# Attention block beside an MLP on one core: which engine empties the second fill bank and which copies the attention output

## The chip, the cores and the metric

The kernel runs on one core of a Trainium2 chip. The core has a matrix engine (TensorE, PE in the profile; its weight loads are shown apart as PEld), a vector engine (VectorE, DVE), an activation engine (ScalarE, ACT), a general engine (GpSimd, POOL) and a queue engine that issues transfers (SyncE, SP). Each engine works through its own list of instructions in order and waits at the head of that list when something it needs is not ready. The metric is the time of one execution on the device in microseconds (us), as the median of several runs.

## What is computed

The input x has 2048 tokens of 512 values. It is layer-normalised; one branch is sliding-window attention with 32 heads of 16 values, the other a normalised MLP with a gate; the result is x plus their product.

```python
xn = layernorm(x)
q, k, v = split(xn @ wqkv)                       # 32 heads, head size 16
scores = q @ k.T * 16 ** -0.5                    # only 0 <= i - j < 256
s = softmax(scores) @ v                          # then (...) @ wo
h = gelu(layernorm(xn) @ w1 + b1)                # 512 -> 1792
g = silu(h @ w2 + b2)                            # 1792 -> 512
out = x + (s @ wo) * g
```

Products are made as three passes over a high and a low part of each operand (`PASSES`, L67), so that the result keeps more bits than one pass gives.

## The kernel before, in words

**Slots.** The attention part is written as one loop over 128 slots, `for t in range(-16, end + 1)` (L816). The heads are handled in 8 groups of 4 (n), and the tokens in 16 blocks of 128 (qb or kb), so slot t stands for group t // 16 and block t % 16. Within a group of four heads the heads go in two pairs, p = 1 and p = 0. Every engine's instructions stay in the order in which the program issues them (L32 to L46), so the order inside a slot is the order on each engine:

1. `prob_block(t, p = 1)` (L548): TensorE makes the scores of one key block against three query blocks into the tile `stb` (two banks of PSUM, the memory that TensorE writes); ScalarE takes their exponentials into a tile `pt`; GpSimd zeroes what lies outside the window (the selects). The scores are 384 columns wide, in the last two blocks of a group 256 and 128.
2. `max_block` (L496) for the slot 12 ahead (`LEAD`, L27): TensorE makes scores into `xy`, VectorE writes the far block from `zo` into it (`copy_predicated`) and takes the row maxima (`tensor_reduce`).
3. `fill_in(t, 0)` (L809): fill matmuls, see below. Then what is planned for the slot by number (`at`).
4. `prob_block(t, p = 0)`: the same as 1, into the same `stb`. So TensorE can only write it when ScalarE has done the exponentials of p = 1.
5. `fill_in(t, 1)`, then `first_scores` (L487) into `zo` for the next slot's maxima.
6. `pv_step` (L570) for the slot before: 24 small matmuls gather probabilities times values into `otb`, a 128-column part of `zo` (L195). A copy moves `otb` to the tile `oraw` (L581), of which every fourth is sent to memory.
7. What is put behind the slot (`behind`), transfers above all.

Line 581 also carries an order for the buffers of `pt` (8 of them, so four slots deep, L64): this copy is made to wait for the exponentials and selects of the slot three back (L582 to L585), so that ScalarE's next exponential, behind it, may write in their place.

**Fill pairs.** TensorE's spare time in the slots is filled with the projections of later groups (`pair_qk`, L363), the values of the second half of the heads (`pair_v`, L413) and the first MLP products (`pair_h`, L425). `tandem` (L440) runs two such jobs at once, in two PSUM banks fb0 and fb1, one job on the upper and one on the lower 64 rows of the array, over slots t0 to t1. The next pair normally starts in slot t1 + 1 with both banks, so both have to be emptied by then. That is done in slot t1, in `fill_in(t1, 0)`: ScalarE copies fb0, VectorE copies fb1 (L470, L471). VectorE's copy stands behind its maxima of slot t1. There are 22 pairs. 20 of them end below slot 116 (the last with 12 slots to go), at t1 = 8, 14, 19, 24, 30, 35, 41, 47, 53, 58, 63, 68, 74, 79, 84, 90, 98, 104, 110 and 115 (L736 to L744). Slots 14, 30 and 110 have scores of 256 columns, 47, 63 and 79 of 128; the other fourteen have 384.

For `pair_qk` the copy goes into a buffer `pjr` of a pool of five (L58), is rounded to a high part `sh` by ScalarE in a later slot, and the rest is subtracted by GpSimd; both are sent by transfers into the rows of the tile `qk` from which scores are made. For `pair_h` the copy `hr` goes to memory. For `pair_v` it goes straight into `vt`.

After slot 128 come the rest of the MLP, the output projection and the gate, which the change does not touch.

Of the kernel before, what the change touches and what calls it, by code (L numbers as in the profile page):

```python
# [18 lines left out]
P = 128  # L19
# [4 lines left out]
NQ = H // 4  # L24
EPS = 1e-5
NEG = -3.0e38
LEAD = 12  # L27
EARLY = 10
ORDER = mybir.DependencyInfo(mybir.DependencyClass.Sync, mybir.DependencyReason.DATA)
# [21 lines left out]
def mixer_kernel(ctx, tc, x, wqk, wv, wo, w1, b1, w2, b2, out):  # L51


    nc = SimpleNamespace(**{name: Ordered(tc, name) for name in ("tensor", "vector", "scalar", "gpsimd", "sync")})
# [140 lines left out]
    otb = zo[:, 1, 256:384]  # L195
    psf = attn.enter_context(tc.tile_pool(name="psf", bufs=1, space=PSUM))
    fb = [psf.tile([P, 512], F32, name=f"fb{i}") for i in range(2)]
# [92 lines left out]
    fills = {}  # L290
# [116 lines left out]
        taken.add(t)  # L407
        return t

    taken = set()  # L410
    among = {}

    def pair_v(i):  # L413
# [26 lines left out]
    def tandem(t0, t1, one, two, mid=None, back=None):  # L440

        n = one[0]
        lo, hi = slice(0, 64), slice(64, P)
        mid = mid or max(1, (t0 + t1 + 1) // 2)
        most = n // 4

        def places(slots, last):

            last = min(most, n // (len(slots) + 1)) if last else 0
            cuts = [(n - last) * k // len(slots) for k in range(len(slots) + 1)]
            out = []
            for t, a, b in zip(slots, cuts, cuts[1:]):
                ahead = min(b - a, 5 * n // 12) if t < 16 * NQ - LEAD else min(b - a, max(most, (b - a + 1) // 2))
                out += [(t, 0)] * ahead + [(t, 1)] * (b - a - ahead)
            return out + [(t1, 0)] * last

        first, second = places(range(t0, mid), False), places(range(back or mid, t1), True)
        for phase, where in enumerate((first, second)):  # L460
            for i in range(n):
                flags = dict(start=(phase == 0 and i == 0), stop=(phase == 1 and i == n - 1), skip_group_check=True)
                def unit(i=i, phase=phase, flags=flags):
                    made = ((two if phase == 0 else one)[1](fb[1 - phase], i, hi, **flags),
                            (one if phase == 0 else two)[1](fb[phase], i, lo, **flags))
                    if phase == 1 and i == 0 and t0 < 16 * NQ - LEAD:
                        for r in made:
                            tc.add_manual_dep(r.ins, outs["copy"].ins.name, ORDER, reason="the banks change rows")
                fills.setdefault(where[i], []).append((unit, ()))
        fills.setdefault((t1, 0), []).append((one[2], (fb[0], t1, nc.scalar.copy)))  # L470
        fills[t1, 0].append((two[2], (fb[1], t1, nc.vector.tensor_copy)))  # L471

    def spread(jobs, places):

# [93 lines left out]
    outs = {}  # L568

    def pv_step(n, qb):  # L570

        lo = max(qb - 2, 0)
        for kb in range(lo, qb + 1):
            for j in range(4):
                nc.tensor.matmul(otb[32 * j: 32 * j + DH + 1], vt[:, kb, (4 * n + j) % 16],
                                 pts[n, kb, j // 2][:, j % 2, P * (qb - kb): P * (qb - kb + 1)],
                                 start=(kb == lo), stop=(kb == qb),
                                 skip_group_check=True, tile_position=(0, 32 * j))
        if qb % 4 == 0:
            outs[0] = sgp.tile([P, 512], F32, tag="or", name=f"oraw_{n}_{qb}", bufs=2)  # L580
        outs["copy"] = nc.scalar.copy(outs[0][:, P * (qb % 4): P * (qb % 4 + 1)], otb)  # L581
        old = 16 * n + qb - 2  # L582
        if old >= 0:
            for w in writers[old // 16, old % 16, 0] + writers[old // 16, old % 16, 1]:
                tc.add_manual_dep(outs["copy"].ins, w.ins.name, ORDER, reason="the next slot writes in its place")  # L585
        if qb % 4 == 3:
            (at if n or qb > 7 else behind)(16 * n + qb + 2, nc.sync.dma_start, oT_d[n // 2, n % 2::2, :, P * (qb - 3): P * (qb + 1)], outs[0])

# [112 lines left out]
    n, raw = raws["qk"]  # L701
# [32 lines left out]
    fills[0, 1].insert(0, fills[0, 0].pop())  # L734
    soon = {}
    tandem(3, 8, pair_qk(1, 2), pair_qk(1, 3))  # L736
    for n, spans in enumerate((((9, 14), (15, 19)), ((20, 24), (25, 30)), ((31, 35), (36, 41)), ((42, 47), (48, 53, 51)),
                               ((75, 79), (80, 84)), ((85, 90), (93, 98))), 2):
        for c, span in zip((0, 2), spans):
            tandem(*span[:2], pair_qk(n, c), pair_qk(n, c + 1), *span[2:])  # L740
    for i, (t0, t1) in enumerate(((54, 58), (59, 63), (64, 68), (69, 74))):
        tandem(t0, t1, pair_v(2 * i), pair_v(2 * i + 1))
# [73 lines left out]
    for t in range(-16, end + 1):  # L816
# [25 lines left out]
        if t >= 1:  # L842
            pv_step((t - 1) // 16, (t - 1) % 16)
# [34 lines left out]
    for f in range(6, NF, 2):  # L878
        t = gp.tile([P, 2, 512], F32, tag="ohl", name=f"hr_{f}", bufs=4)
# [453 lines left out]
```

## Time and profile before

| what | value |
|---|---|
| median of 3 runs | 746.3 us (746.1 to 747.39) |
| profiled execution, its own time | 746.44 us |
| its span, first to last instruction | 744.7 us |
| VectorE busy | 516.5 us (69%) |
| ScalarE busy | 439.8 us (59%) |
| GpSimd busy | 298.6 us (40%) |
| granted TensorE clock | 0.999 |
| attention slots 0 to 127 | about 62 to 430 us |

The profile is of one execution. In lists of instructions a row gives the start and the duration in us, the engine, the operation, what is written and read, the shapes, and how many like it are merged; a bracket tells how long the engine sat idle before it and what ended that. Lists by group give the count, the busy time in us, the mean of one in ns, and the idle time before. A list of waits gives the total in us, the number of times and, where there is a third number, the longest.

### The profile page before, as it was taken

How to read it: one execution, taken by the hardware profiler on the slowest of the kernel's cores; microseconds unless marked ns; L12 is line 12 of the kernel's file. 1: busy time of each engine (PE TensorE's matmuls, PEld its weight loads, DVE VectorE, ACT ScalarE, POOL GpSimd, SP SyncE). 2: the span in 40 equal slices, each digit the busy share in tenths (PEclk: the TensorE clock that was granted, in tenths of full speed). 3: DMA queues.
4: the chain of work that ended last, by engine and by line, in shares of the span. 5: the costliest groups of instructions: out<-in, count | busy, mean ns of one | idle time of the engine just before them, and what ended most of it. 6: DMA issues, size and time to landing. Idle time of an engine off the chain costs nothing.

```text
span 744.7 us, 18740 instructions
## 1 busy us (share of the span) xinstructions
PE 728.3 (98%) x7360; PEld 587.2 (79%) x7360; DVE 516.5 (69%) x790; ACT 439.8 (59%) x744; POOL 298.6 (40%) x644
## 2 busy tenths in 40 slices
PE   8999999999999999999999999999999999999997
PEld 7886777777778888777776688788888888888886
DVE  6886777877776678887772577656658855676643
ACT  7757767867667676778877856443544734442001
POOL 7413757757666555767867600020102000001102
PEclk9999999999999999999999999999999999999999
DMA  8633356666555625656735385746453222254711
GB/s 294 188 71 78 86 136 149 188 173 190 147 133 154 152 71 152 156 135 168 199 102 159 102 285 196 196 142 194 109 109 113 98 87 74 68 182 116 218 50 57
DMA packets 84025, 105.71 MB, mean 142 GB/s; under 512 B 36640, under 2 KB 36896, under 8 KB 83936
## 3 DMA queue, kind: packets, MB, share of 16 engines
q1 hardware_dynamic: 83936, 104.50, 49.8%
q8 instruction: 58, 0.95, 0.5%
q14 instruction: 31, 0.25, 0.1%
HBM read 54.53 MB, written 32.77 MB: 117 GB/s over the span
## 4 chain that ended last, share of the span: by engine, by line
PE 87%; DMA 4%; ACT 4%; DVE 3%; issue 1%; POOL 1%; SPq 1%; DVEq 0%; ACTq 0%
PE fb L43 19%; PE acc L43 17%; PE zo L43 12%; PE p L43 9%; PE stb L43 9%; PE s L43 6%; PE h L43 6%; PE xy L43 5%; PE pv L43 3%; ACT pt L43 3%; DMA w<-rden_d 1%; POOL pt L43 1%; SPq L43 1%; DVE xy L43 1%; DMA qk<-qk 1%
## 5 line engine op out<-in xcount | busy, mean ns | idle before, releaser
L43 POOL TENSOR_SCALAR_AFFINE_SELECT pt<-pt 128x256 f32<-128x256 f32 x480 | 193.8, 428 | 131.7 <-ACT pt L43 127.5
L43 ACT ACTIVATE pt<-stb 128x768 f32<-128x768 f32 (+1 forms) x244 | 188.7, 773 | 56.0 <-PE stb L43 50.3
L43 DVE TENSOR_REDUCE mt<-xy 128x4 f32<-128x1024 f32 (+1 forms) x128 | 152.6, 1192 | 4.4
L43 DVE COPY_PREDICATED xy<-upper,zo 128x512 f32<-128x512 int32 x112 | 77.8, 695 | 69.9 <-PE xy L43 60.9
L43 POOL TENSOR_TENSOR xo<-xo,gated 128x512 f32<-128x512 f32 x15 | 20.0, 1331 | 237.3 <-DVE gated L43 195.7
L43 PE MATMUL fb<-xnT,wqb 64*128 64x512 f32 (+1 forms) x684 | 105.2, 399 | 0.4
L43 PE MATMUL zo<-pt,vt 128*17 128x128 f32 x2880 | 103.7, 275 | 0.3 <-POOL pt L43 0.3
L43 PE MATMUL stb<-qk 64*128 64x384 f32 (+1 forms) x488 | 94.6, 383 | 6.0 <-ACT pt L43 4.3
L43 PE MATMUL acc<-w,gh 128*128 128x512 f32 x320 | 98.6, 389 | 0.8 <-ACT gh L43 0.8
L43 PEld LDWEIGHTS stb<-qk 64*128 64x128 f32 x488 | 45.8, 183 | 47.6 <-ACT pt L43 41.4
L43 PEld LDWEIGHTS zo<-pt,vt 128*17 128x17 f32 x2880 | 67.5, 97 | 15.7 <-issue 5.7
L43 PEld LDWEIGHTS fb<-xnT,wqb 64*128 64x128 f32 (+1 forms) x684 | 64.6, 185 | 11.9 <-DVE pjr L43 1.6
L43 PEld LDWEIGHTS acc<-w,gh 128*128 128x128 f32 x320 | 60.0, 188 | 13.5 <-ACT gh L43 1.2
L43 PE MATMUL acc<-w,gl 128*128 128x512 f32 x160 | 62.3, 390 | 1.0 <-DVE gl L43 1.0
L43 PE MATMUL xy<-qk 64*128 64x256 f32 (+2 forms) x536 | 58.3, 291 | 0.2 <-DVE mt L43 0.2
L43 ACT COPY oraw<-zo 128x128 f32<-128x128 f32 x128 | 34.1, 267 | 35.2 <-PE zo L43 23.8
L43 PEld LDWEIGHTS xy<-qk 64*128 64x128 f32 x536 | 46.6, 185 | 6.7 <-issue 3.4
L43 PE MATMUL s<-wos,ohl 128*128 128x512 f32 (+1 forms) x204 | 44.3, 376 | 0.0
L43 ACT ACTIVATE gated<-acc 128x512 f32<-128x512 f32 x16 | 8.7, 596 | 59.3 <-DVE acc L43 59.3
L43 PEld LDWEIGHTS s<-wos,ohl 128*128 128x128 f32 x204 | 36.8, 188 | 7.1
L43 PEld LDWEIGHTS zo<-qk 64*128 64x128 f32 x448 | 37.6, 185 | 5.0 <-DVE xy L43 1.8
L43 ACT COPY p<-p 128x512 f32<-128x512 f32 x21 | 12.3, 585 | 48.6 <-PE p L43 41.3
(191 smaller groups left out, 1235.2 us busy)
## 6 DMA issues: line engine op xcount, KB each, us to landing
qk<-sh SPq DMA_DIRECT2D x128, 128.0 KB
qk<-pjr SPq DMA_DIRECT2D x64, 128.0 KB
oT_d<-oraw SPq DMA_DIRECT2D x32, 256.0 KB
w_d<-in_w_dram SPq DMA_DIRECT2D x14, 512.0 KB
x<-in_x_dram SPq DMA_DIRECT2D x16, 256.0 KB
or<-oT_d SPq DMA_DIRECT2D x16, 256.0 KB
w<-rden_d SPq DMA_DIRECT2D x16, 256.0 KB
xo<-in_x_dram SPq DMA_DIRECT2D x16, 256.0 KB
```

The source lines that it names most:

```text
L43: r = issue(*args, **kwargs)
```

## The change

In the 20 slots in which a pair ends below slot 116, two copies change engine and place. The copy of the second bank fb1 goes from VectorE, ahead of the p = 0 exponentials, to ScalarE, behind them (`fill_in(t1, 1)`). The copy of that slot's `otb` goes from ScalarE to VectorE. The order that protects the `pt` buffers moves from the `otb` copy to the new copy of fb1, since it has to stand on ScalarE. The two pairs that end at 116 or later, 121 and 127, stay as they were.

```diff
-    taken = set()
+    taken, ends_pair = set(), set()
...
         fills.setdefault((t1, 0), []).append((one[2], (fb[0], t1, nc.scalar.copy)))
-        fills[t1, 0].append((two[2], (fb[1], t1, nc.vector.tensor_copy)))
+        if t1 >= 16 * NQ - LEAD:
+            fills[t1, 0].append((two[2], (fb[1], t1, nc.vector.tensor_copy)))
+            return
+        ends_pair.add(t1)
+
+        def copy(dst, src):
+            outs["second"] = nc.scalar.copy(dst, src)
+        fills.setdefault((t1, 1), []).append((two[2], (fb[1], t1, copy)))
...
-        outs["copy"] = nc.scalar.copy(outs[0][:, P * (qb % 4): P * (qb % 4 + 1)], otb)
-        old = 16 * n + qb - 2
+        t = 16 * n + qb + 1
+        by = nc.vector.tensor_copy if t in ends_pair else nc.scalar.copy
+        outs["copy"] = by(outs[0][:, P * (qb % 4): P * (qb % 4 + 1)], otb)
+        last = outs["second" if t in ends_pair else "copy"]
+        old = t - 3
         if old >= 0:
             for w in writers[old // 16, old % 16, 0] + writers[old // 16, old % 16, 1]:
-                tc.add_manual_dep(outs["copy"].ins, w.ins.name, ORDER, reason="the next slot writes in its place")
+                tc.add_manual_dep(last.ins, w.ins.name, ORDER, reason="the next slot writes in its place")
```

On ScalarE the list of such a slot was: exponentials p = 1, copy of fb0, exponentials p = 0, copy of `otb`. It becomes: exponentials p = 1, copy of fb0, exponentials p = 0, copy of fb1. On VectorE the copy of fb1 (128 x 512) gives way to the copy of `otb` (128 x 128). In the built program the order of every other instruction on all engines is the same, apart from which buffer of the pool of five some tiles get. In slot 8 ScalarE also rounds the first bank's copy right behind the new copy.

## Prediction

> **What bounds the kernel now.** I read the page first, then the list of waits, then the places of the 20 slots in order of time. The page says that TensorE is the engine that is never free; the waits say what still holds it up.
>
> ```profile
> PE 728.3 (98%) x7360; PEld 587.2 (79%) x7360; DVE 516.5 (69%) x790; ACT 439.8 (59%) x744; POOL 298.6 (40%) x644
> ```
> ```profile
> PEld stb L43 <- ACT pt L43: 41.4, 144, 0.7
> ```
> ```profile
>   DVE pjr L43: 1.9, 9
>   DVE hr L43: 0.9, 3
>   DVE vt L43: 0.2, 1
> ```
>
> The second row is the loop of the attention: TensorE waits for ScalarE's exponentials before it can write `stb` again. The last three (waits at the fill matmuls, by the tile fb) are what this change can reach: 3.0 us in 13 cases in which a new pair stood waiting for VectorE's copy of fb1. Idle time of the weight loads is not yet lost time, so I went to the slots themselves. Slot 41, where a pair ends, and slot 42:
>
> ```profile
> 183.07 0.59 ACT L43 COPY pjr<-fb 128x512 f32<-128x512 f32 x1
> 183.17 1.23 DVE L43 TENSOR_REDUCE mt<-xy 128x4 f32<-128x1024 f32 x1
> ...
> 183.55 0.82 ACT L43 ACTIVATE pt<-stb 128x768 f32<-128x768 f32 x1
> ...
> 184.31 0.68 DVE L43 COPY pjr<-fb 128x512 f32<-128x512 f32 x1
> ...
> 184.52 0.27 ACT L43 COPY oraw<-zo 128x128 f32<-128x128 f32 x1 [0.15 <-PE zo L43]
> 184.53 0.36 PEld L43 LDWEIGHTS xy<-qk 64*128 64x128 f32 x4
> ...
> 184.90 0.81 ACT L43 ACTIVATE pt<-stb 128x768 f32<-128x768 f32 x1
> 185.04 0.76 PEld L43 LDWEIGHTS fb<-xnT,wqb 64*128 64x128 f32 x8 [0.15 <-DVE pjr L43]
> ...
> 185.19 0.70 DVE L43 COPY_PREDICATED xy<-upper,zo 128x512 f32<-128x512 int32 x1 [0.21 <-PE xy L43]
> ...
> 186.46 0.81 ACT L43 ACTIVATE pt<-stb 128x768 f32<-128x768 f32 x1 [0.74 <-PE stb L43]
> ```
>
> VectorE is in its maxima until 184.40, copies fb1 until 184.99, and the fill starts at 185.04. A slot without that wait and with the same 8 fill matmuls is slot 43:
>
> ```profile
> 187.43 0.36 PEld L43 LDWEIGHTS xy<-qk 64*128 64x128 f32 x4
> 187.72 0.78 PEld L43 LDWEIGHTS fb<-xnT,wqb 64*128 64x128 f32 x8
> ```
> ```profile
> 187.80 0.81 ACT L43 ACTIVATE pt<-stb 128x768 f32<-128x768 f32 x1
> 189.17 0.81 ACT L43 ACTIVATE pt<-stb 128x768 f32<-128x768 f32 x1 [0.56 <-PE stb L43]
> ```
>
> From the `xy` loads to the fill it takes 0.29 us there, 0.51 in slot 42; from the first to the second exponentials 1.37 there, 1.56 in slot 42. So the wait costs up to 0.19 us in that slot. Of a gap between exponentials about 1.35 is the loop's own least (183.55 to 184.90), whatever the fill does; what lies above it can be won.
>
> **ScalarE's new copy.** Let X be the start of the p = 0 exponentials in the ending slot. When can the copy start, and when is ScalarE free for the next exponentials? Rows with a copy out of PSUM right behind exponentials:
>
> ```profile
> 307.88 0.82 ACT L43 ACTIVATE pt<-stb 128x768 f32<-128x768 f32 x1
> ...
> 308.58 0.27 ACT L43 COPY oraw<-zo 128x128 f32<-128x128 f32 x1
> ```
>
> The copy starts 0.70 after the exponentials, 0.12 before they end. In slot 41 the exponentials follow the fb0 copy by 183.55 - 183.07 = 0.48. So the new copy runs from X + 0.70 to X + 1.29 (0.59 as fb0's), the fill may go at X + 1.34 (0.05 from copy to fill, as 184.99 to 185.04), and ScalarE is free at X + 1.18. The next exponentials need their scores and start at X + 1.35, so the copy is hidden in ScalarE's gap with 0.17 to spare; without that cover it would cost its whole 0.59 less the 0.27 taken away, 0.32 a pair or 6.4 us in 20. The copy has its waits met: fb1's last matmul lies before the p = 0 exponentials, the selects and exponentials of three slots back are old, and its buffer's transfers were done where VectorE came to it:
>
> ```profile
> L43 DVE COPY pjr<-fb 128x512 f32<-128x512 f32 x13 | 8.8, 680 | 0.0
> ```
>
> (idle before: 0.0.) Behind it in ScalarE's queue stand the next exponentials, and for these TensorE waits.
>
> [...]
>
> **VectorE's new copy.** No row shows a 128 x 128 copy out of PSUM on VectorE. It lies above the transpose of 32 columns (202 ns) and below the 680 ns of the wide copy; I take 0.29 us, near ScalarE's 267 ns for the same shape, the nearest row.
>
> ```profile
> L43 DVE STREAM_TRANSPOSE mT<-mh 128x32 f32<-128x32 f32 x30 | 6.1, 202 | 0.7 <-POOL mh L43 0.7
> L43 ACT COPY oraw<-zo 128x128 f32<-128x128 f32 x128 | 34.1, 267 | 35.2 <-PE zo L43 23.8 <-POOL pt L43 4.0 <-POOL mh L43 2.4
> ```
>
> It waits for the matmuls into `otb`, behind which ScalarE's copy started at 184.52; VectorE's maxima end at 184.40, so it is done near 184.8. Behind it stand a small transpose in some slots and the next `copy_predicated`, which needs `xy` and starts at 185.19; TensorE needs `otb` only a slot later. So it costs nothing at either end of its range: even at 0.68 VectorE is as busy as now. VectorE's load falls by some 20 x 0.39 = 7.8 us, ScalarE's rises by 6.4. Nothing else moves in the queues of SP and GpSimd; their transfers of these copies only become ready earlier.
>
> **The sum, by three kinds of slots.** Wide scores (384): fill from X + 1.34 in place of where it starts now. Slot 41: 183.55 + 1.34 = 184.89 against 185.04, so 0.15. The first and the last of this kind:
>
> ```profile
> 134.83 0.82 ACT L43 ACTIVATE pt<-stb 128x768 f32<-128x768 f32 x1
> ...
> 136.35 0.76 PEld L43 LDWEIGHTS fb<-xnT,wqb 64*128 64x128 f32 x8 [0.19 <-DVE pjr L43]
> ```
> ```profile
> 396.41 0.82 ACT L43 ACTIVATE pt<-stb 128x768 f32<-128x768 f32 x1
> ...
> 397.90 0.19 PEld L43 LDWEIGHTS fb<-yh,xnT 64*128 64x128 f32 x2 [0.41 <-DVE hr L43]
> ```
>
> They give 0.18 and 0.15. There are nine (24, 35, 41, 53, 58, 74, 98, 104, 115), read the same way at 0.12 to 0.18: 9 x 0.14 = 1.3 us. In the five others (8, 19, 68, 84, 90) the next fill does not wait or the next gap is already the loop's least; slot 8 has the wait, but slot 9 reads
>
> ```profile
> 89.40 0.81 ACT L43 ACTIVATE pt<-stb 128x768 f32<-128x768 f32 x1
> 90.74 0.81 ACT L43 ACTIVATE pt<-stb 128x768 f32<-128x768 f32 x1 [0.53 <-PE stb L43]
> ```
>
> 1.34: nothing to win. Narrow scores (256; slots 14, 30, 110): the exponentials are shorter, so the copy comes earlier, while VectorE's maxima are as long as ever. Slot 14 and an unhindered narrow slot:
>
> ```profile
> 104.93 0.60 ACT L43 ACTIVATE pt<-stb 128x512 f32<-128x512 f32 x1
> ...
> 105.82 0.30 PEld L43 LDWEIGHTS xy<-qk 64*128 64x128 f32 x4
> ...
> 106.42 1.00 PEld L43 LDWEIGHTS fb<-xnT,wqb 64*128 64x128 f32 x10 [0.30 <-DVE pjr L43]
> ```
> ```profile
> 245.13 0.30 PEld L43 LDWEIGHTS xy<-qk 64*128 64x128 f32 x4
> ...
> 245.36 0.79 PEld L43 LDWEIGHTS fb<-wva,xnT 64*128 64x128 f32 x12
> ```
>
> Copy from 104.93 + 0.48 (0.60 less the overlap) to 106.00, fill at 106.05; TensorE is ready 0.23 after the `xy` loads, also 106.05. Against 106.42 that is 0.37, and 3 x 0.36 = 1.1. Scores of 128 (47, 63, 79):
>
> ```profile
> 200.10 0.39 ACT L43 ACTIVATE pt<-stb 128x256 f32<-128x256 f32 x1
> ...
> 200.99 0.36 PEld L43 LDWEIGHTS xy<-qk 64*128 64x128 f32 x4
> ...
> 201.59 0.76 PEld L43 LDWEIGHTS fb<-xnT,wqb 64*128 64x128 f32 x8 [0.24 <-DVE pjr L43]
> ```
>
> The copy would be done by 201.0, so the fill goes 0.29 after `xy`, at 201.28: 0.3 each. Slot 79 has two casts on ScalarE behind it that fill the gap, so I count 47 and 63: 0.6. The sum is 1.3 + 1.1 + 0.6 = 3.0 us off the profiled execution's 746.44, which is 0.1 above the median: 743.4. What follows in the loop is timed from the slot before it, so I expect nothing to be given back; next in line is the loop of `stb` and exponentials itself.
>
> **Rivals.** *The wait only changes its name* (time 746.3). In the chain of waits slot 42 shows no gap, the fill follows the `xy` matmuls at once:
>
> ```profile
> 184.86 0.24 PE xy L43 x4
> 185.10 1.15 PE fb L43 x8
> ```
>
> If the weight loads alone waited, nothing is won. Against it: 1.56 against 1.37 for the same work. The same comes out if copy and exponentials do not overlap: with 0.05 at each handing over, the next exponentials would start at X + 0.82 + 0.05 + 0.59 + 0.05 = X + 1.51. The five slots at the loop's least lose 0.16 each (0.8), the nine lose 0.03 (fill at 1.51 against 1.48, 0.3), the narrow ones still win 3 x 0.2 + 2 x 0.3 (1.2): 746.3. [...]
>
> *The copy stands at ScalarE's head and holds up the exponentials* (749). It takes over waits that the `otb` copy had: the row above has 4.0 us of idle time put down to selects (POOL pt). It decides from the point where the copy starts later than X + 0.87, where the case without overlap comes out even; each 0.1 us beyond is 0.1 in 20 slots, 2 us. At 0.14 beyond, X + 1.01, it is 2.8 us slower. For it: ScalarE's idle gap is only 0.17 wide. Against it: those selects are three slots old, and the idle rows lie where `otb` itself ends.
>
> **Chances.** Forecast 0.62, nothing won 0.24 (0.14 for the name alone, 0.10 for no overlap), slower 0.14. About 0.2% or 1.5 us is what a measurement of this kernel can tell from no change; the forecast is beyond that. Faster 0.62, same 0.24, slower 0.14. If the whole of the delay at the fills goes (0.19 to 0.22 in the nine), the sum is 3.7, so 742.2 with a little for the run; above, the range takes in the second case and the start of the third: 742.2 to 747.2.
>
> **What would show it.** Right: the fill rows by tile fb wait for neither VectorE nor ScalarE beyond a tenth; the fb1 copies on ScalarE start 0.70 behind the exponentials; gaps from X to the next exponentials stay at 1.35; the gaps one slot on fall from 1.56 to about 1.41; in slot 15 the fill starts 0.23 behind the `xy` loads, not 0.60; VectorE's 20 narrow copies take near 0.29. Wrong: idle time at fb1 copies on ScalarE, gaps of 1.4 to 1.5 at the pair's end, or fill waits put down to ACT.

## The result and the profile after

The changed kernel takes **742.66 us** (median of 6 runs, 742.09 to 743.89) against 746.22 for the kernel before in the same session (6 runs, 744.93 to 747.53): a ratio of 0.9951, with a 95% interval of 0.9937 to 0.9965, so 3.6 us less. The profiled execution took 742.66 us, with a span of 740.9 where before it was 744.7, at a granted clock of 0.998.

The page of the changed kernel, its engines' row, and from its list of waits the loop's own wait:

```profile
PE 724.8 (98%) x7360; PEld 586.4 (79%) x7360; DVE 509.9 (69%) x790; ACT 444.0 (60%) x744; POOL 297.8 (40%) x644
```
```profile
PEld stb L43 <- ACT pt L43: 41.6, 143, 0.7
```

TensorE is busy 3.5 us less with the same 7360 matmuls (3.0 of it in slots 0 to 127), so the time that rows of matmuls cover is not work alone. The wait for the exponentials is what it was, 41.6 us against 41.4: the change did not touch the loop of scores and exponentials. In the waits at the fill matmuls (by the tile fb of the changed kernel) the three VectorE rows are gone. Two waits for a copy of fb are left, both for ScalarE:

```profile
  ACT hr L43: 0.5, 2
```

One of them, at 421.3, belongs to the pair that ends in slot 127. The other is that of slot 115, which the change does reach: its fill waits 0.27 us for ScalarE's copy, where it waited 0.41 for VectorE's (397.90 in the rows of the prediction).

```profile
394.20 0.19 PEld L43 LDWEIGHTS fb<-yh,xnT 64*128 64x128 f32 x2 [0.27 <-ACT hr L43]
```

The groups by shape of the changed kernel show the copies at their new places (count, busy us, mean ns, idle before):

```profile
L43 ACT COPY oraw<-zo 128x128 f32<-128x128 f32 x108 | 28.7, 266 | 30.9 <-PE zo L43 18.8 <-POOL pt L43 4.7 <-POOL mh L43 3.5
L43 ACT COPY pjr<-fb 128x512 f32<-128x512 f32 x28 | 16.5, 590 | 3.1 <-PE fb L43 1.8 <-DMA qk<-qk 0.4
L43 DVE COPY oraw<-zo 128x128 f32<-128x128 f32 x20 | 5.8, 290 | 2.0 <-PE zo L43 0.8
```

Slots 41 and 42 of the changed kernel, in order of time:

```profile
181.38 0.59 ACT L43 COPY pjr<-fb 128x512 f32<-128x512 f32 x1
...
181.86 0.82 ACT L43 ACTIVATE pt<-stb 128x768 f32<-128x768 f32 x1
...
182.56 0.59 ACT L43 COPY pjr<-fb 128x512 f32<-128x512 f32 x1
182.80 0.29 DVE L43 COPY oraw<-zo 128x128 f32<-128x128 f32 x1
...
183.21 0.79 PEld L43 LDWEIGHTS fb<-xnT,wqb 64*128 64x128 f32 x8
183.32 0.81 ACT L43 ACTIVATE pt<-stb 128x768 f32<-128x768 f32 x1 [0.16 <-PE stb L43]
...
184.67 0.81 ACT L43 ACTIVATE pt<-stb 128x768 f32<-128x768 f32 x1 [0.54 <-PE stb L43]
```

With X = 181.86 the second bank's copy runs from X + 0.70 to X + 1.29, and the fill starts at X + 1.35 with no wait in its row. VectorE has emptied `otb` at 183.09, 0.47 before the next `copy_predicated` (183.56). In this one slot the scores came 0.1 late (next exponentials at X + 1.46; in the other eight of its kind 1.35 to 1.38), so the gain of slot 42 (1.56 to 1.35 from one exponentials to the next) is in part taken back here. TensorE waits there for a transfer (last section). Slots 14 and 15 of the changed kernel, the narrow kind:

```profile
104.74 0.60 ACT L43 ACTIVATE pt<-stb 128x512 f32<-128x512 f32 x1
...
105.23 0.59 ACT L43 COPY pjr<-fb 128x512 f32<-128x512 f32 x1
...
105.63 0.30 PEld L43 LDWEIGHTS xy<-qk 64*128 64x128 f32 x4
...
105.87 0.99 PEld L43 LDWEIGHTS fb<-xnT,wqb 64*128 64x128 f32 x10
```

The fill stands 0.24 behind the `xy` loads; it was 0.60 (105.82 to 106.42 in the rows of before).

To put the gain in places I took the time from the first exponentials of an ending slot to those two slots later, after less before, and summed it by the prediction's kinds; "rest" is every other slot of the 128. These columns are against the first profile of before; each ratio is to runs of before of the same session, with medians from 745.56 to 746.22. The last two kernels are told of under "What lies outside the pairs".

| kernel | median us, ratio to before [95%] | nine wide | six narrow | five at the loop's least | rest |
|---|---|---|---|---|---|
| the change | 742.66, 0.9951 [0.9937, 0.9965] | -1.20 | -1.92 | +0.18 | -0.67 |
| fb1_only | 743.59, 0.9964 [0.9952, 0.9976] | -1.24 | -1.97 | +0.31 | -0.67 |
| otb_only | 746.04, 1.0004 [0.9994, 1.0014] | +0.04 | +0.20 | +0.35 | -0.86 |
| fb1_ahead | 748.81, 1.0039 [1.0024, 1.0055] | +1.98 | -0.41 | +2.12 | -0.46 |
| narrow_only | 743.6, 0.9969 [0.996, 0.9978] | -0.06 | -2.16 | -0.03 | -0.09 |
| wide_only | 744.1, 0.998 [0.9971, 0.9989] | -0.91 | -0.18 | +0.27 | -0.41 |
| fb1_twice | 753.62, 1.0106 [1.009, 1.0123] | +4.67 | +1.24 | +3.17 | -0.95 |
| best1 | 742.14, 0.9954 [0.9941, 0.9966] | -0.70 | -1.96 | +0.06 | -0.32 |
| before, second profile | one run, 746.3 | -0.04 | +0.03 | -0.03 | -0.16 |
| before_plus2 | 746.44, 1.001 [0.9999, 1.0022] | -0.02 | -0.14 | +0.06 | -0.47 |
| before_plus5 | 746.06, 1.0003 [0.9994, 1.0013] | +0.23 | +0.05 | +0.19 | -0.47 |

The pairs of the change sum to -2.93 us, where the prediction had 3.0. The rest, -0.67, it did not have.

### The profile page after: what moved, and what is told of

The parts are those of the page before. It is cut to its first block, busy times and chain, and to the rows that moved or that the text cites. A ratio compares the mean times of both kernels' runs of the same rounds, so it can differ in the third digit from the quotient of the medians.

```text
span 740.9 us, 18755 instructions
## 1 busy us (share of the span) xinstructions
PE 724.8 (98%) x7360; PEld 586.4 (79%) x7360; DVE 509.9 (69%) x790; ACT 444.0 (60%) x744; POOL 297.8 (40%) x644
## 4 chain that ended last, share of the span: by engine, by line
PE 86%; DMA 4%; ACT 4%; DVE 3%; SPq 1%; POOL 1%; issue 1%; DVEq 0%; ACTq 0%
PE fb L43 18%; PE acc L43 18%; PE zo L43 13%; PE p L43 9%; PE stb L43 9%; PE s L43 6%; PE h L43 6%; PE xy L43 5%; PE pv L43 3%; ACT pt L43 3%; DMA qk<-sh 1%; DMA w<-rden_d 1%; SPq L43 1%; POOL pt L43 1%; DMA qk<-qk 1%
## 5 line engine op out<-in xcount | busy, mean ns | idle before, releaser
L43 PEld LDWEIGHTS stb<-qk 64*128 64x128 f32 x488 | 45.9, 183 | 48.4 <-ACT pt L43 41.6
L43 ACT COPY oraw<-zo 128x128 f32<-128x128 f32 x108 | 28.7, 266 | 30.9 <-PE zo L43 18.8
L43 ACT COPY p<-p 128x512 f32<-128x512 f32 x21 | 12.3, 584 | 48.6 <-PE p L43 41.4
```

The lines of the kernel that those rows point to most:

```text
L43: r = issue(*args, **kwargs)
```

## The experiments

The theory: in the slot where a pair ends, the fill of the next pair waits for the second bank; with ScalarE's copy behind its exponentials the fill can start 0.14 to 0.36 us sooner than with VectorE's behind its maxima, and ScalarE has just room for it. The rivals: the gain is VectorE's lighter load or the move of `otb`; or it is somewhere else than in the pairs. The diffs are against the changed kernel unless said otherwise.

**Each half alone.** In fb1_only the `otb` copy stays on ScalarE, behind the new copy:

```diff
-        by = nc.vector.tensor_copy if t in ends_pair else nc.scalar.copy
+        by = nc.scalar.copy
...
-        last = outs["second" if t in ends_pair else "copy"]
+        last = outs["copy"]
```

> The fb1 copy goes to ScalarE behind the p = 0 exponentials as in the change, but the otb copy stays on ScalarE behind it. My theory (the gain is the fill's shorter wait for fb1): fills start as in the change, X + 1.35 in wide slots and X + 1.13 or 1.2 in narrow ones; ScalarE's list is 0.18 longer in the gap, so the next exponentials move from X + 1.35 to between X + 1.36 and X + 1.40 in 14 wide slots: 743 to 743.5 us, at least three quarters of the gain. Rival (the gain is otb going to VectorE, out of ScalarE's way): the gain is gone, 746. Rival (the gain is VectorE's lighter load): VectorE loses 13.6 us instead of 7.8, so as fast as the change or faster, 742 to 742.7.

In otb_only the second bank goes back to VectorE ahead of the p = 0 exponentials, and the order of the `pt` buffers to the copy of the first bank:

```diff
-        fills.setdefault((t1, 0), []).append((one[2], (fb[0], t1, nc.scalar.copy)))
+        def copy(dst, src):
+            outs["second"] = nc.scalar.copy(dst, src)
+        fills.setdefault((t1, 0), []).append((one[2], (fb[0], t1, copy)))
+        fills[t1, 0].append((two[2], (fb[1], t1, nc.vector.tensor_copy)))
         if t1 >= 16 * NQ - LEAD:
-            fills[t1, 0].append((two[2], (fb[1], t1, nc.vector.tensor_copy)))
             return
         ends_pair.add(t1)
-
-        def copy(dst, src):
-            outs["second"] = nc.scalar.copy(dst, src)
-        fills.setdefault((t1, 1), []).append((two[2], (fb[1], t1, copy)))
```

> Only the otb copy changes to VectorE in the 20 slots; the fb1 copy stays on VectorE behind its maxima. The order for the pt buffers is moved to ScalarE's fb0 copy. My theory: fills start as before (X + 1.49), nothing won; VectorE has 0.29 more in front of its next maxima, 0 to 0.1 in each of 20 slots: 746 to 747.5 us. Rival (otb out of ScalarE's way is the gain): 743 to 744.

fb1_only took 743.59 us, a ratio of 0.9964 [0.9952, 0.9976]; otb_only 746.04, 1.0004 [0.9994, 1.0014]. So the gain is that of the earlier copy of fb1, and the move of `otb` brings nothing by itself. A lighter VectorE is not the gain either: in fb1_only it copies neither in these slots, and the time is no shorter than that of the change.

otb_only is not a clean half. With the order on the copy of fb0, ScalarE's sequencer goes through two more waits ahead of that copy, and the p = 0 exponentials come up to 0.18 us later behind those of p = 1 (in slot 41 1.54, where before has 1.41). The fill of the next pair is not moved by that: in slot 41 it starts 2.90 behind the p = 1 exponentials in both kernels, so it still goes by VectorE's copy.

Slot 41 in fb1_only:

```profile
181.83 0.82 ACT L43 ACTIVATE pt<-stb 128x768 f32<-128x768 f32 x1
182.53 0.59 ACT L43 COPY pjr<-fb 128x512 f32<-128x512 f32 x1
183.00 0.30 ACT L43 COPY oraw<-zo 128x128 f32<-128x128 f32 x1
183.17 0.76 PEld L43 LDWEIGHTS fb<-xnT,wqb 64*128 64x128 f32 x8
183.18 0.83 ACT L43 ACTIVATE pt<-stb 128x768 f32<-128x768 f32 x1
```

Even both copies fit: the second starts 0.47 behind the first, at X + 1.17, and the exponentials follow at X + 1.35 as in the change. Only in slot 8, where ScalarE rounds a copy in the same gap as well, does it cost: the next exponentials come at X + 1.85, in the change at X + 1.69 (1.70 before). The move of `otb` to VectorE is cover for such a slot, and the runs show no more of it: the intervals of fb1_only and of the change overlap, and their pairs sum to -2.90 and -2.93.

**The copy ahead of the exponentials.** ScalarE copies both banks one after the other between p = 1 and p = 0:

```diff
-        fills.setdefault((t1, 1), []).append((two[2], (fb[1], t1, copy)))
+        fills[t1, 0].append((two[2], (fb[1], t1, copy)))
```

> As the change, but ScalarE copies fb1 right behind fb0, ahead of the p = 0 exponentials. VectorE's load is that of the change. My theory: the fill never waits, but the exponentials come 0.48 later in all 20 slots; nine wide slots lose 0.48 - 0.2, five lose 0.48, six narrow ones lose about 0.12: 751 to 752.5 us. Rival (VectorE's lighter load is the gain): 742 to 743.

It took 748.81 us, 1.0039 [1.0024, 1.0055]. Slot 41 of fb1_ahead, with the two copies in one row:

```profile
182.63 0.81 ACT L43 ACTIVATE pt<-stb 128x768 f32<-128x768 f32 x1
...
183.56 1.07 ACT L43 COPY pjr<-fb 128x512 f32<-128x512 f32 x2
...
184.52 0.83 ACT L43 ACTIVATE pt<-stb 128x768 f32<-128x768 f32 x1
```

From p = 1 to p = 0 it is 1.89 where it was 1.41, and nothing hides the 0.48. The fill then never waits for a copy, and yet eight of the nine wide slots lose 0.26 to 0.40 each against before. Slot 115 alone wins 0.42; the first scores behind it go to `xy` and do not wait for `stb`. VectorE's load is that of the change, so this run speaks against the rival of the lighter VectorE too. The direction was as expected, but the time is 2.2 us below the least expected, 751. I had charged the six narrow slots 0.12 each, 0.7 in all, and they came out 0.41 ahead. There the 0.48 comes back in two parts: in slots 14 and 30 0.38 at the fill that no longer waits and 0.10 in a shorter gap after the p = 0 exponentials, in 47 and 63 about 0.3 at each. Slot 115, charged 0.28, accounts for 0.7 more. So the early copy was a loss in the wide slots inside the loop; behind the exponentials, where ScalarE waits anyway, it was none.

**Narrow and wide slots apart.** The change only where the scores are 256 or 128 wide, then only where they are 384:

```diff
-        if t1 >= 16 * NQ - LEAD:
+        if t1 % 16 < 14 or t1 >= 16 * NQ - LEAD:
```

> The change in the six narrow slots alone (14, 30, 47, 63, 79, 110). My theory: they give 0.1 to 0.36 each, together 1.7 to 2.0 us: 744.3 us, half or more of the gain from 6 of 20 slots. Rival (a gain that goes with the number of copies moved, as VectorE's load does): 6/20 of 3.6, 1.1 us: 745.1. The sum over the slots of the profile tells these apart, as the times may not.

```diff
-        if t1 >= 16 * NQ - LEAD:
+        if t1 % 16 > 13 or t1 >= 16 * NQ - LEAD:
```

> The change only in the 14 ending slots with scores of 384 columns. Theory: the nine that waited win 1.2 us, the five at the loop's least lose up to 0.2, so 1.0 us below before, near 745.2; together with the narrow slots alone (2.3 in the slot sums) that makes the change's 3.5. Rival: the gain lies in the six narrow slots alone, and here the time is that of before, 746.2, with a pair sum between -0.3 and 0.3.

narrow_only took 743.6 us, 0.9969 [0.996, 0.9978], wide_only 744.1, 0.998 [0.9971, 0.9989]. In shares of before these are 0.31% and 0.20%, together 0.51%; the change has 0.49%. The two kinds add up, and the kind not changed stays still in each (-0.06 and -0.03 in narrow_only; -0.18 in wide_only, of which 0.16 lies in slot 110 and follows a loss of 0.18 in slot 109). The -2.16 of narrow_only holds 0.21 of the same sort, won in slot 63 after slot 62 lost 0.25. Both come from late copies, told below. The -0.91 of wide_only lacks 0.30 that slot 41 lost to a late transfer (last section). Six narrow slots bring more than nine wide ones, as the prediction's terms said (1.7 and 1.3). The rival that the wide slots give nothing falls; against the before of its own session (745.56) wide_only is 1.5 us lower where 1.0 was expected; its slots sum to -1.2.

**A second copy behind the first.** To see how much room ScalarE has, it copies the second bank twice, to the same place:

```diff
         def copy(dst, src):
+            nc.scalar.copy(dst, src)
             outs["second"] = nc.scalar.copy(dst, src)
```

> In every ending slot ScalarE copies the second bank twice, to the same place, which adds one 128 x 512 copy behind the first. Theory: the first copy had 0.17 us to spare, so the second is on the path. It starts at X + 1.17 and ends at X + 1.76, the next exponentials follow it by 0.48, at X + 1.65 in place of 1.35, and the fill starts at X + 1.81. Against before: nine slots +0.3 each and five +0.4, the three of 256 columns +0.3, those of 128 about 0: some 5.6 us, so 752 (751 to 753). Rival: ScalarE's gap is wider than the rows say and takes a second copy beside TensorE's work; then only the fill is late, by 0.3 us against before in nine slots, and the time is 748 to 749 or less.

It took 753.62 us, 1.0106 [1.009, 1.0123], 8.1 us above the before of its session (745.56) where 5.6 was expected. Slot 41 of fb1_twice:

```profile
185.50 0.82 ACT L43 ACTIVATE pt<-stb 128x768 f32<-128x768 f32 x1
...
186.20 1.27 ACT L43 COPY pjr<-fb 128x512 f32<-128x512 f32 x2
...
187.37 0.82 ACT L43 ACTIVATE pt<-stb 128x768 f32<-128x768 f32 x1
187.52 0.76 PEld L43 LDWEIGHTS fb<-xnT,wqb 64*128 64x128 f32 x8 [0.68 <-ACT pjr L43]
```

The two copies take 1.27 where two to different places took 1.07 in fb1_ahead: the second starts 0.68 behind the first, 0.09 after its end, at X + 1.39 (1.38 in the other wide slots). The trace shows why. The second writes what the first writes, and between the two ScalarE's sequencer has a wait for a semaphore that ScalarE itself raises; it ends at X + 1.35, and the copy starts 0.04 later. So the delay is a wait in the program. The exponentials follow at X + 1.87 or 1.86, that is 0.48 behind that start, in place of 1.35; the fill is at X + 2.02. The nine wide slots lose 0.49 to 0.53 each where 0.3 was expected, the five others 0.51 to 0.74, the three of 256 columns 0.31 to 0.33 and the three of 128 about 0.1. That makes 9.1 in the pairs, 8.1 with the -0.95 of the rest.

The theory had the start of the second copy wrong, and its rule right: the next exponentials came 0.48 after the start of the last 128 x 512 copy, or when their scores let them, whichever was later (1.38 to 1.86 in wide slots, 1.17 to 1.65 with 256 columns, 0.96 to 1.44 with 128). In a wide slot a copy at X + 0.70 gives 1.18 and is free. By the same sum (1.35 less 0.48, an estimate) a copy costs from a start at X + 0.87 on; no run has one that starts there.

**What lies outside the pairs.** Is the rest of -0.67 the first profile's own? The kernel before, unchanged, profiled again:

> The kernel before, profiled a second time. In the first comparison the 128 slots shortened by 3.60 us, 2.93 of it in the 20 pairs; 0.67 lay in slots that the change does not touch. If that 0.67 belongs to the first profile of before, this profile's slots outside the pairs are shorter by 0.4 to 0.9 us and the pairs themselves stay within 0.3 us. If the change shortens other slots too, the two profiles of before agree within 0.2 us outside the pairs.

It moved -0.04 in the pairs and -0.16 in the rest, 0.12 of that in slot 12. So 0.12 of the 0.67 was the first profile's. Another 0.54 lies in four slots: 16, 17, 38 and 39 are 0.14, 0.14, 0.11 and 0.15 shorter in the change, and by about the same in nearly every edited kernel, even those that leave the pairs near them alone. Slot 16 in the second profile of before shows where it was lost:

```profile
111.23 0.85 PE L43 MATMUL zo<-pt,vt 128*17 128x128 f32 x24
112.47 0.27 ACT L43 COPY oraw<-zo 128x128 f32<-128x128 f32 x1 [0.72 <-PE stb L43]
112.63 0.82 ACT L43 ACTIVATE pt<-stb 128x768 f32<-128x768 f32 x1
```

The matmuls into `otb` end at 112.08, but ScalarE's copy starts 0.39 later, and the exponentials behind it with it. Usually it is about 0.1. I counted ScalarE's list in the trace, with the waits that its sequencer executes as instructions of their own. The wait ahead of this copy is number 190, and those of the two other late copies, in slots 38 and 88, are 318 and 574. In these three the copy begins 0.32 after the wait has ended, in 96 others of the first profile of before 0.04 (exceptions such as 0.16 in slots 49, 97 and 113 and 0.34 in slot 118 are the same in the change). The change, like every edit here, adds or moves such waits and so shifts the numbers. To test that, before gets two or five copies of one column on ScalarE, long ahead of slot 0 (`range(5)` in before_plus5):

```diff
     nc.vector.memset(negc, NEG)
+    scr = const.tile([P, 1], F32, name="scr")
+    for _ in range(2):
+        nc.scalar.copy(scr, upper[:, :1])
```

> The kernel before with two copies of one column on ScalarE put in long before slot 0; nothing else is changed. In the traces so far a copy of otb that ScalarE enters straight from its wait for TensorE begins 0.04 us after the wait, but 0.32 where the wait is instruction 62, 126, 190 and so on of ScalarE's list (a step of 64), which in before are slots 16, 38 and 88. Theory: ScalarE takes its list in blocks of 64, and the first of a block that comes straight out of a wait starts 0.28 late. With two instructions more, no such copy lies at a block's edge in slots 0 to 127: the 0.32 at slots 16, 38 and 88 becomes 0.04, slots 16 and 17 shorten by 0.26 together and 38 and 39 by 0.27, and the time falls by 0.5 us (745.1 to 745.8 against 746.2). Rival: those slots wait for TensorE or a transfer, and the same three copies are late by 0.28 again, with the time of before.

> The same with five such copies. Theory: the blocks' edges now fall on the copies of otb in slots 15, 37, 49 and 75, which begin 0.32 after their wait in place of 0.04, and those in slots 16, 38 and 88 begin 0.04 after it. The time stays within 0.5 us of before, since some slots win 0.26 and others lose up to as much. Rival: the late copies stay in slots 16, 38 and 88.

In before_plus2 the three copies are on time (slots 16 and 17 shorter by 0.13 each, 38 and 39 by 0.24 together, against the second profile of before), here slot 16:

```profile
111.11 0.85 PE L43 MATMUL zo<-pt,vt 128*17 128x128 f32 x24
112.08 0.27 ACT L43 COPY oraw<-zo 128x128 f32<-128x128 f32 x1 [0.44 <-PE zo L43]
112.39 0.81 ACT L43 ACTIVATE pt<-stb 128x768 f32<-128x768 f32 x1
```

In before_plus5 the copies in slots 15 and 37 are late by the same amount, as expected; slot 15:

```profile
108.05 0.85 PE L43 MATMUL zo<-pt,vt 128*17 128x128 f32 x24
109.30 0.27 ACT L43 COPY oraw<-zo 128x128 f32<-128x128 f32 x1 [1.20 <-PE stb L43]
```

Those in 49 and 75 are not (0.16 and 0.04), and this mends the theory: 190, 318 and 574 are 62 more than 128, 256 and 512, and the waits of slots 49 and 75 in before_plus5 are 382 and 510, which lie half-way between. So the step is 128 and not 64. Over all twelve profiles 16 of the waits ahead of a copy of `otb` lie at 62 above a multiple of 128, and every one is followed by a copy 0.32 late, in whichever slot it falls. That the late start moves with the number and not with the slot is shown. Why it is 128 is not shown, and that ScalarE takes its list in blocks, as the expectations have it, was the author's guess.

In time it can't be seen. before_plus2 took 746.44, 1.001 [0.9999, 1.0022], where 0.5 less was expected; the interval leaves no room for that, and this expectation failed. before_plus5 took 746.06, 1.0003 [0.9994, 1.0013]. The trace of before_plus2 is 0.37 shorter than the second one of before from the first to the last exponentials, and 0.34 longer behind them; that last part, which no edit touches, spreads from 319.1 to 320.4 us over the twelve profiles. So the 0.54 stands in the slots of the change's trace, as a by-product of a list that is counted differently, but whether it is a part of the 3.6 us in time stays open. The pairs alone make 2.9.

**A version without the small losses.** Slots 68 and 84 left as before, and in slot 121 both banks on VectorE:

```diff
-        fills.setdefault((t1, 0), []).append((one[2], (fb[0], t1, nc.scalar.copy)))
-        if t1 >= 16 * NQ - LEAD:
+        fills.setdefault((t1, 0), []).append((one[2], (fb[0], t1, nc.vector.tensor_copy if t1 == 121 else nc.scalar.copy)))
+        if t1 in (68, 84) or t1 >= 16 * NQ - LEAD:
```

> The change without slots 68 and 84, where VectorE's copy was early and the pair lost 0.06 and 0.09 us, and with both banks of the pair that ends in slot 121 on VectorE, since there ScalarE's copy of the first bank stands 0.47 us between two exponentials and TensorE has one stall of 0.28 us behind that chain. Theory: 0.15 and up to 0.28, so 0.2 to 0.45 us less than the change, 742.3 or so. Rival: GpSimd's selects are the bound in slots 121 to 124, and the change's 742.7 stays as it is. A difference of 0.4 us is about what these rounds can tell; the rows at 121 decide.

It took 742.14 us (5 runs), 0.9954 [0.9941, 0.9966]: beside the change's 0.9951 no difference can be told. Slots 68 and 84 give 0.09 back together. Behind slot 121 little is won: the exponentials of slot 122 follow those of slot 121 by 2.02 us in both kernels, slot 122 is 0.33 longer and slots 124 and 125 are 0.29 and 0.19 shorter, -0.15 for slots 122 to 125. The rival, GpSimd's selects as the bound there, is not ruled out: the copy of `otb` ahead of the exponentials of slot 122 waits 0.53 for a select in best1 and 0.54 in the change. The profile of best1 also has two losses to late transfers, 0.45 in slot 33 and 0.5 more than the change in slot 41, so its slot sums are worse than its time.

## Why the prediction was right, point by point

- *ScalarE's new copy.* Start at X + 0.70, end at X + 1.29, fill at X + 1.34, exponentials at X + 1.35: measured 0.70, 1.29 to 1.30, 1.35 (1.38 in slot 35) and, in the nine wide slots, 1.35 to 1.38 (once 1.46). The spare of 0.17 was the step that decided, and fb1_twice shows what a copy past it costs.
- *No overlap.* The prediction's second way to 746.3 had copy and exponentials one behind the other, with the next exponentials at X + 1.51. No run shows that: copy and exponentials overlap by 0.12 in each of the wide pairs (start at X + 0.70, exponentials of 0.82), two copies to different places start 0.48 apart with 0.59 each (fb1_ahead), and the time was 742.66.
- *VectorE's new copy.* 0.29 us, as taken; the end of the range at 0.68 was not needed. By groups VectorE lost 20 copies of 0.68 and gained 20 of 0.29, as said. The busy time of the page moved less than the 7.8 and 6.4 us of the prediction (VectorE 6.6 down, ScalarE 4.2 up), since neighbouring rows overlap and the page counts the overlap once: added up row by row, VectorE lost 8.0 (542.2 to 534.2) and ScalarE gained 6.3 (467.3 to 473.6).
- *Wide slots.* 9 x 0.14 = 1.3 expected, 1.20 measured: seven gave 0.12 to 0.16, slot 41 gave 0.10 and slot 35 0.08. TensorE comes to the fill of slot 35 only at X + 1.38 (1.39 in fb1_ahead, where the copy was long done).
- *256 columns.* 3 x 0.36 = 1.1 expected; each gave 0.35, so 1.05.
- *128 columns.* 0.6 expected in 47 and 63; they gave 0.27 and 0.29. Slot 79 was counted at nothing because of two casts on ScalarE behind it, and gave 0.29 as well: the exponentials behind the casts came 1.74 after those ahead of them, where it had been 1.86, so the casts had not filled the gap. This gain was put at nothing wrongly.
- *The five others.* Nothing expected, 0.18 lost, in 68 (0.06) and 84 (0.09) above all. The prediction asked only whether there was something to win in these, not whether the new place is later than the old. Slot 68 of the kernel before:

```profile
261.22 0.69 DVE L43 TENSOR_REDUCE mt<-xy 128x4 f32<-128x512 f32 x1
...
261.65 0.82 ACT L43 ACTIVATE pt<-stb 128x768 f32<-128x768 f32 x1
261.83 0.68 DVE L43 COPY vt<-fb 128x512 f32<-128x512 f32 x1
...
262.91 1.03 PEld L43 LDWEIGHTS fb<-wva,xnT 64*128 64x128 f32 x16
```

  The maxima there take 0.69 and not 1.23 (half the columns), so VectorE was done at X + 0.86 and the fill went at X + 1.26, when TensorE was ready. In the change it waits for ScalarE until X + 1.35:

```profile
258.94 0.81 ACT L43 ACTIVATE pt<-stb 128x768 f32<-128x768 f32 x1
259.64 0.59 ACT L43 COPY vt<-fb 128x512 f32<-128x512 f32 x1
...
260.29 1.01 PEld L43 LDWEIGHTS fb<-wva,xnT 64*128 64x128 f32 x16
```

- *The sum.* 3.0 expected, 2.93 in the pairs; the errors of slot 79 (0.29 too little), the five (0.18 too much) and the wide ones (0.1 too much) cancel, so that the two agree this well is in part luck. That nothing is given back held: the next in line was the loop of scores and exponentials, whose wait did not move. The time itself fell by 3.56 us, 0.5 more than the forecast 3.0; the 0.54 of slots 16, 17, 38 and 39, which the prediction did not have, is of that size, with its standing as told above.
- *The signs.* The gaps one slot on fell as said, and slot 15 has its fill 0.24 behind the `xy` loads. One sign failed: at slot 115 the fill waits 0.27 for ScalarE, more than the tenth allowed, and the slot still gained 0.14. The gap of 1.46 in slot 41, of a size that the prediction named as a sign of being wrong, comes from a transfer (last section) and not from the copy.
- *Rivals.* "The wait only changes its name" fell with the gaps of slot 42 and its kind (nine gaps shorter by 0.08 to 0.20). "The copy stands at ScalarE's head" is real in fb1_twice (second copy at X + 1.38, next exponentials at X + 1.87 or 1.86), but by the estimate above only from a start at X + 0.87 on; at X + 0.70 the next exponentials came at 1.35 to 1.38.

## What to carry to other kernels

When two engines can empty a bank, ask of each when it is free in that slot, not how long its copy takes: here ScalarE, which waits anyway for the next step of the loop, took a copy of 0.59 us for nothing, since its start plus 0.48 (X + 1.18) lay before the time at which the loop came back to it (X + 1.35). The same copy 0.7 us earlier, on the loop's path, put the exponentials back by 0.48, and eight of the nine wide slots lost 0.26 to 0.40 (fb1_ahead). And read the exceptions off the trace slot by slot: where VectorE's reduction was short, the old place was the better one.

## What the runs showed of the hardware that was not expected

- On ScalarE a copy of `otb` that comes straight out of a wait whose number in the list, counted with the sequencer's waits, is 62 above a multiple of 128 starts 0.28 us late (0.32 after the wait in place of 0.04, 16 of 16 cases). Other instructions at such places were not tested. In before that falls on slots 16, 38 and 88, in the change on slot 86, in before_plus5 on 15 and 37. Why this is so is not shown.
- Two 128 x 512 copies on ScalarE to different places start 0.48 apart, though each takes 0.59 (fb1_ahead). The 0.68 of two copies to the same place in fb1_twice is a wait in the program and no sign of the engine.
- In four profiles TensorE came late to the scores behind slot 41: the change, wide_only, best1 and before_plus5 have the next exponentials at X + 1.46, 1.75, 1.96 and 1.84 in place of 1.35. As the last of these is the kernel before with five small copies, the change is not the cause. TensorE's sequencer waits there for the transfer that brings the row maxima into `qk` (`qk<-mT_d`): in the four it lands at X + 0.84, 1.14, 1.34 and 1.23, in the first profile of before at X - 0.54. The loss of best1 in slot 33 is the same wait. Why the transfer is later in these executions is open.
